# A planner that lays out the opening too, knows the shared port, picks engines, and fills TensorE's gaps with zero products

## The chip, the cores and the metric

The kernel runs on one core of one Trainium2 chip. The metric is the device time of one execution in microseconds (us), the median of several runs. The engines are TensorE (PE, matrix products; PEld is its weight load), VectorE (DVE), ScalarE (ACT), GpSimd (POOL) and SyncE (SP, which here only issues DMAs).

## The reference

An mLSTM layer runs over 4 batches, 8 heads, 768 steps and a head dimension of 40; its output, 3072 rows of 320, goes through a bilinear block of width 1536. All arrays are float32 but the three weight matrices, which come as 8-byte floats.

```
for t in range(S):
    m_new = max(f_gate[t] + m, i_gate[t])
    f_stab = exp(f_gate[t] + m - m_new);  i_stab = exp(i_gate[t] - m_new);  m = m_new
    C = f_stab * C + i_stab * outer(v[t], k[t])
    n = f_stab * n + i_stab * k[t]
    denom = max(abs(n . q[t]), 1)
    y[t] = sigmoid(o_gate[t]) * (C @ q[t]) / denom
x = y as (B*S, H*D)
out = ((x @ w_a) * (x @ w_b)) @ w_out
```

## The kernel before

The recurrence is computed chunkwise: 24 chunks of 128 steps (6 per batch, batches interleaved). For a chunk, `begin_a`/`stage_a` make transposed q and k (tile T), `begin_e`/`stage_e` a matrix of decays (E, tile gbc), `begin_b`/`stage_b` the scores (pS) times E, `begin_i`/`stage_i` the part of the carried state (pI), `begin_c`/`stage_c` the product with v (pV), `stage_u` the state's update (pU from vw), `stage_f` the division and gate (tile osig becomes y) and `stage_d` the transposed result, split in two floats of shorter mantissa (xh, xl). The first six chunks use the `begin_` forms, float32 products; later ones use split bf16.

The bilinear block (`moe_block`) takes the chunks in 9 blocks of 2, 2, 3, 3, 3, 3, 3, 2 and 3 chunks. For each of 12 slices of the width, `up` makes two sums of 8 products (pu, 256 or 384 columns, three PSUM buffers), copies one (g), multiplies it by the other, splits g into gh and gl; `down`, two slices later, adds three products per chunk into pd0, pd1, pd2 (320 columns). The last slice copies pd to o and stores it.

The weights come as 8-byte floats in 32 stages. Each stage is made into two floats in the kernel: `high` and `low` read the raw words (qks and cw), `join` puts them together (DVE), `lead_part` copies the leading part (w), `low_part` subtracts it (DVE). The products of the first block wait for them.

The order of the work is made by a planner, `Plan`. The kernel's code is run against a recorder; each call becomes a `Node` with its engine, an occupancy and a latency from `cost`, and edges from `link`: data, ring buffers of a tile, and, while `plan.pinned` is set, the order as written on each engine. `run` is a list scheduler: per engine the ready node of the best rank goes first; `settle` runs it forward and backward 6 times (TURNS), and `emit` issues every engine's instructions in the best order found. All instructions therefore carry one line number in the profile (L349), and tiles tell them apart. Pinned before were the first loads and the hand-written opening: up to the first two chunks' `stage_d` and the first five weight stages. Behind them, PE, DVE and ACT were free, and every later node came after the last pinned one of its engine.

In `run`, SP's loads share one wire with 8 in flight (LANES). Ten products of zeros (`warm`, in bank pd2) stand at the start to raise TensorE's clock.

Of the kernel before, what the change touches and what calls it, by code (L numbers as in the profile page):

```python
# [22 lines left out]
LANES = 8  # L23

# [75 lines left out]
class Node:  # L100
    __slots__ = (
        "i", "eng", "calls", "occ", "lat", "prev", "next", "table", "acc", "pinned", "at", "done", "xfer",
    )

    def __init__(self, i, eng):
        self.i, self.eng, self.calls, self.prev, self.next = i, eng, [], {}, []
        self.occ = self.lat = self.xfer = 0.0
        self.table, self.acc, self.pinned = None, [], False


class Plan:

    ENGINES = {"tensor": "PE", "vector": "DVE", "scalar": "ACT", "gpsimd": "POOL", "sync": "SP"}
    HOP = 0.07

    def __init__(self, nc):
        self.nc, self.nodes, self.rings, self.pinned = nc, [], {}, True
        for name in self.ENGINES:  # L120
            setattr(self, name, Recorder(self, name))

# [3 lines left out]
    def add(self, engine, op, args, kw):  # L126
        eng = self.ENGINES[engine]
# [12 lines left out]
        if not (  # L140
            eng == "PE" and node is not None and node.eng == "PE" and node.acc[0][0] == okey
            and len(node.calls) < 8 and node.pinned == self.pinned
        ):
            node = Node(len(self.nodes), eng)
            node.pinned = self.pinned
            self.nodes.append(node)
        node.calls.append((engine, op, args, kw))
        node.acc += acc
        self.cost(node, eng, op, out, refs, args, kw)
# [17 lines left out]
    def cost(self, node, eng, op, out, refs, args, kw):  # L167
        cols = int(np.prod(out.shape[1:]))
        size = [x.size if isinstance(x, View) else mybir.dt.size(x.dtype) for x in refs]
        if eng == "PE":  # L170
            if op == "transpose":
                occ = 0.109
            else:
                f32 = [str(x.dtype) if not isinstance(x, View) else x.kind() for x in refs[1:3]]
                if size[1] == 2:
                    occ = cols / 2400 + 0.005 if cols > 64 else 0.026
                elif "float32r" in f32[0]:
                    occ = cols / 2400 + 0.011
                else:
                    occ = 0.108 if refs[1].shape[0] <= 64 else 0.22  # L180
            node.occ += occ
            node.lat = 0.17
        elif eng == "ACT":
# [3 lines left out]
            node.occ = 0.04 + cols * 0.00094 + (0.13 if bias else 0.0)  # L187
            node.occ += 0.05 if "Prelu" in func or "scale" in kw else 0.0
            node.lat = 0.11
        elif eng == "DVE":  # L190
            rate = 960.0
            one = op in ("tensor_copy", "tensor_scalar", "memset") and all(
                not isinstance(x, View) or x.root.ring[0] != "psum" for x in refs
            )
# [4 lines left out]
            node.occ = 0.065 + cols / rate  # L199
            node.lat = 0.085  # L200
        elif eng == "POOL":
            node.occ = 0.1 + cols * (0.0009 if op in ("affine_select", "memset") else 0.002)
            node.lat = 0.1
        elif op == "dma_start_transpose":
            node.occ, node.lat, node.xfer = 1.3, 1.6, 0.0
        else:
            n = int(np.prod(out.shape)) * size[0]
            rows = out.shape[-1] * size[0]
            node.occ, node.lat = 0.47 if rows > 512 else 0.6, 1.7
            node.xfer = n / (340e3 if rows > 512 else 172e3)  # L210

    def link(self):
        last, chain, rings = {}, {}, {}
        for node in self.nodes:
# [22 lines left out]
        for node in self.nodes:  # L237
            if not node.pinned and node.eng in ("PE", "DVE", "ACT"):
                self.edge(chain[node.eng], node, order=True)
# [7 lines left out]
    def edge(self, a, b, order=False):  # L247
        if a is b or (order and a.i in b.prev):
            return
        if a.eng == b.eng and a.eng != "SP":  # L250
            gap = a.occ
            if a.eng in ("DVE", "ACT", "POOL") and not order:
                gap += 0.06
        else:
            gap = a.occ if order else None
        if order and a.eng != b.eng:
            gap = 0.0
        if a.i not in b.prev:
            a.next.append(b)
            b.prev[a.i] = gap  # L260
        elif gap is None or (b.prev[a.i] is not None and gap > b.prev[a.i]):
            b.prev[a.i] = gap

    def run(self, rank, forward=True):
        nodes = self.nodes
        engines = list(dict.fromkeys(self.ENGINES.values()))
        free = dict.fromkeys(engines, 0.7 if forward else 0.0)
        wait = {e: [] for e in engines}
# [4 lines left out]
        table, wire, landed = "E", 0.0, []  # L273
        order = []
        for x in nodes:
            if lack[x.i] == 0:
                heapq.heappush(wait[x.eng], (0.0, rank[x.i], x.i))
        while len(order) < len(nodes):
            best = None
            for e in engines:  # L280
                if ready[e]:
                    t = free[e]
                elif wait[e]:
                    t = max(free[e], wait[e][0][0])
                else:
                    continue
# [3 lines left out]
            while wait[e] and wait[e][0][0] <= t + 1e-9:  # L290
                r, k, i = heapq.heappop(wait[e])
                heapq.heappush(ready[e], (k, i))
            k, i = heapq.heappop(ready[e])
            x = nodes[i]
            if x.table and x.table != table:
                table = x.table
                t += 1.283
            at[i] = t
            free[e] = t + x.occ
            if e == "SP":  # L300
                if forward:
                    if len(landed) >= LANES:
                        t = max(t, landed[-LANES])
                    at[i], free[e] = t, t + x.occ
                    wire = max(wire, t + x.lat) + x.xfer if x.xfer else wire
                    end[i] = wire + 0.35 if x.xfer else t + x.occ + x.lat
                    landed.append(end[i])
                else:
                    free[e] = t + max(x.occ, x.xfer)
                    end[i] = t + x.occ + x.lat + x.xfer  # L310
            else:
                end[i] = t + x.occ + x.lat
            order.append(x)
            for y in x.next if forward else [nodes[j] for j in x.prev]:
                lack[y.i] -= 1
                if lack[y.i] == 0:
                    r = 0.0
                    if forward:
                        for j, gap in y.prev.items():
                            r = max(r, end[j] + self.HOP if gap is None else at[j] + gap)  # L320
                    else:
                        for z in y.next:
                            gap = z.prev[y.i]
                            r = max(r, at[z.i] + z.occ + (y.lat + self.HOP if gap is None else gap - y.occ))
                    heapq.heappush(wait[y.eng], (r, rank[y.i], y.i))
        return order, at, max(end)

    def settle(self):
# [3 lines left out]
        for turn in range(TURNS):  # L332
            order, at, end = self.run(rank)
            if best is None or end < best[1]:
                best = (order, end, at)
            back, late, _ = self.run([-t for t in at], forward=False)
            rank = [-(t + x.occ) for t, x in zip(late, self.nodes)]
# [4 lines left out]
    def emit(self, order):  # L342
# [3 lines left out]
        for node in order:  # L346
            for engine, op, args, kw in node.calls:
                f = getattr(getattr(self.nc, engine), op)
# [7 lines left out]
class Recorder:  # L356

    def __init__(self, plan, name):
        self._plan, self._name = plan, name

    def __getattr__(self, op):
        return lambda *args, **kw: self._plan.add(self._name, op, args, kw)
# [17 lines left out]
def kernel(  # L380
# [395 lines left out]
    def stage_a(n):  # L776
# [10 lines left out]
        for j in range(2):  # L787
            qks = qks2[2 * (n % 2) + j]
            ph, pm, pl = (qks[:, 1, :, at[i][j]:at[i][j] + D] for i in "hml")
            nc.scalar.copy(ph, src[:, j])  # L790
# [3 lines left out]
            (nc.gpsimd if 2 * n + j < 4 else nc.vector).tensor_tensor(r, src[:, j], ph, op=ALU.subtract)  # L794
            nc.vector.tensor_copy(pm, r)
            yield
            (nc.gpsimd if n < 8 else nc.vector).tensor_tensor(pl, r, pm, op=ALU.subtract)
# [21 lines left out]
    def stage_b(n, hf):  # L819
# [14 lines left out]
        nc.scalar.copy(pb[:, 0], E)  # L834
# [115 lines left out]
    def stage_f(n):  # L950
# [15 lines left out]
        (nc.vector if n < NS else nc.gpsimd).tensor_tensor(  # L966
# [4 lines left out]
        (nc.scalar.copy if n < NF32 else nc.vector.tensor_copy)(y[:, DM:], y[:, 2 * P:DM])  # L971
# [5 lines left out]
    def stage_d(n):  # L977
# [15 lines left out]
        nc.scalar.copy(xh[:, :, cols], px)  # L993
# [65 lines left out]
    def moe_block(kb):  # L1059
# [5 lines left out]
        def down(ff):  # L1065
# [13 lines left out]
            if ff == NF - 1:  # L1079
                for t in range(sizes[kb]):  # L1080
# [3 lines left out]
                    nc.scalar.copy(o, pd[t][:, 0:DM])  # L1084
                    nc.sync.dma_start(out[b * S + c * P:b * S + (c + 1) * P, :], o)

        def up(ff):
# [5 lines left out]
            for j in range(2):  # L1093
# [12 lines left out]
                if j == 0:  # L1106
                    g = mpool.tile([P, NTB], F32, tag="acp", name=f"g{kb}_{ff}")[:, 0:NT]
                    (nc.vector.tensor_copy if kb > 0 and ff in [1, 2] else nc.scalar.copy)(g, acc[0])
# [33 lines left out]
    def begin_a(n):  # L1142
# [6 lines left out]
        for j in range(2):  # L1149
# [6 lines left out]
            pool, tag = (ps_at, "pat") if n >= NS or n + j == 0 else (ps_dn, "pd2") if j == 0 else (ps_up, "pu")  # L1156
# [6 lines left out]
            (nc.vector.tensor_copy if j == 1 else nc.scalar.copy)(t, pt)  # L1163
# [99 lines left out]
    plan.pinned = False  # L1263
# [11 lines left out]
    plan.pinned = True  # L1275
# [4 lines left out]
    for _ in range(WARM):  # L1280
        nc.tensor.matmul(warm, idle[:, 0:P], idle, start=True, stop=True)

# [139 lines left out]
```

## Time and profile before

| | |
|---|---|
| median of 3 runs (lowest, highest) | 553.07 us (552.47, 554.78) |
| the profiled execution | 552.61 us, span 550.8 us |
| busy, share of the span | PE 96%, PEld 92%, DVE 74%, ACT 43%, POOL 23% |
| mean granted TensorE clock | 0.966 |
| q, k, v, o_gate loads, 160 KB each | 24 of each |

"Busy" is the share of the span in which an engine had an instruction under way. The clock row of the profile gives the granted clock in tenths of full speed for 40 equal slices of the span, 9 being 90% or more. A name such as pu<-xh,w is output from inputs by the program's tiles.

### The profile page before, as it was taken

The numbers are of one execution on the slowest core, as the hardware profiler recorded it, in microseconds if no ns is written. First come the engines' busy times: TensorE is split into PE (matmuls) and PEld (weight loads), VectorE is DVE, ScalarE is ACT, GpSimd is POOL, SyncE is SP. The second block draws the span as 40 slices with busy tenths as digits, with TensorE's granted clock in tenths as the row PEclk, the third lists the DMA queues.
The fourth block names the chain that finished last, engine by engine and source line by source line (L and its number), as shares of the span: only waits on it lengthen the run. The fifth ranks groups of instructions, "written<-read, shape, count | busy, mean of one in ns | idle before, by whom it ended". The sixth has DMA issues, their size and how long they took to land. (4 is left out here: it accounts for less than half of the span.)

```text
span 550.8 us, 12384 instructions
## 1 busy us (share of the span) xinstructions
PE 529.5 (96%) x4810; PEld 506.3 (92%) x4810; DVE 408.0 (74%) x940; ACT 234.4 (43%) x556; POOL 126.1 (23%) x185
## 2 busy tenths in 40 slices
PE   7787899989999999999999999999999999999997
PEld 5676899989999999999899999999999999999997
DVE  5897875578969985987869985988869856844342
ACT  5689997354523642432623444432432622311111
POOL 2012353453232231242132131232030202000000
PEclk9668799989999999999999999999999999999999
DMA  9999923559767756479745659567635535100001
GB/s 170 304 255 312 163 54 65 150 87 166 149 142 125 159 121 149 96 123 171 134 118 129 100 131 191 91 137 147 120 107 86 115 64 116 38 1 26 1 1 37
DMA packets 198679, 66.77 MB, mean 121 GB/s; under 512 B 184252, under 2 KB 191900, under 8 KB 198620
## 3 DMA queue, kind: packets, MB, share of 16 engines
q1 hardware_dynamic: 198620, 65.98, 58.1%
q8 instruction: 38, 0.62, 0.5%
q14 instruction: 21, 0.17, 0.1%
HBM read 41.11 MB, written 5.97 MB: 85 GB/s over the span
## 5 line engine op out<-in xcount | busy, mean ns | idle before, releaser
L349 PE MATMUL pu<-xh,w 128*128 128x384 f32 (+1 forms) x1080 | 281.5, 328 | 0.6 <-ACT xh L349 0.6
L349 PE MATMUL pu<-xl,w 128*128 128x384 f32 (+1 forms) x648 | 211.9, 329 | 1.0 <-DVE xl L349 1.0
L349 PEld LDWEIGHTS pu<-xh,w 128*128 128x128 f32 x1080 | 195.6, 194 | 1.7 <-ACT xh L349 1.0
L349 PE MATMUL pd<-w,gh 128*128 128x320 f32 x576 | 134.5, 315 | 0.0
L349 PEld LDWEIGHTS pu<-xl,w 128*128 128x128 f32 x648 | 126.0, 194 | 2.1 <-DVE xl L349 1.3
L349 PEld LDWEIGHTS pd<-w,gh 128*128 128x128 f32 x576 | 98.0, 190 | 0.4
L349 DVE TENSOR_TENSOR g<-pu,g 128x384 f32<-128x384 f32 (+1 forms) x108 | 54.7, 507 | 57.9 <-PE pu L349 53.5
L349 PE MATMUL pd<-w,gl 128*128 128x320 f32 x288 | 90.4, 315 | 0.0
L349 ACT COPY g<-pu 128x384 f32<-128x384 f32 (+1 forms) x92 | 40.3, 438 | 96.5 <-PE pu L349 96.3
L349 ACT ACTIVATE gbc<-gbc,gtab 128x128 f32<-128x128 f32 x160 | 54.3, 394 | 20.5 <-POOL gbc L349 20.5
L349 POOL TENSOR_TENSOR vr<-va 128x336 f32<-128x336 f32 x18 | 14.5, 804 | 211.7 <-PE pV L349 211.7
L349 PEld LDWEIGHTS pd<-w,gl 128*128 128x128 f32 x288 | 54.3, 189 | 0.2 <-DVE gl L349 0.2
L349 DVE TENSOR_TENSOR gl<-g,gh 128x384 fp32r<-128x384 f32 (+1 forms) x92 | 51.7, 562 | 1.9
L349 ACT CAST pb<-gbc 128x512 bf16<-128x512 f32 x36 | 22.3, 619 | 45.0 <-DVE gbc L349 44.8
L349 PE MATMUL pV<-va,gbc 128*128 128x42 bf16 (+1 forms) x240 | 36.2, 235 | 1.8 <-ACT T L349 1.8
L349 DVE CAST gh<-g 128x384 fp32r<-128x384 f32 (+1 forms) x96 | 33.9, 353 | 1.7
L349 DVE TENSOR_TENSOR num<-pV,num 128x336 f32<-128x336 f32 x20 | 10.1, 505 | 32.9 <-PE pV L349 32.9
L349 DVE TENSOR_TENSOR gbc<-pS,gbc 128x512 f32<-128x512 f32 x48 | 32.3, 680 | 2.9 <-PE pS L349 2.3
L349 ACT CAST cb<-cst 128x168 bf16<-128x168 f32 x18 | 6.0, 333 | 61.6 <-DVE cst L349 34.2
L349 PE MATMUL pS<-T,T 120*128 120x128 bf16 (+1 forms) x352 | 29.4, 236 | 1.8 <-DVE T L349 1.8
L349 PEld LDWEIGHTS <-T 120*128 120x128 bf16 x576 | 24.7, 97 | 6.4 <-issue 4.1
L349 POOL TENSOR_TENSOR gl<-g,gh 128x256 fp32r<-128x256 f32 x16 | 13.1, 821 | 56.5 <-ACT gh L349 49.7
(102 smaller groups left out, 763.7 us busy)
## 6 DMA issues: line engine op xcount, KB each, us to landing
gbc<-g_dram SPq DMA_DIRECT2D x20, 512.0 KB
qk<-in_q_dram SPq DMA_DIRECT2D x24, 160.0 KB
qk<-in_k_dram SPq DMA_DIRECT2D x24, 160.0 KB
va<-in_v_dram SPq DMA_DIRECT2D x24, 160.0 KB
osig<-in_o_gate_dram SPq DMA_DIRECT2D x24, 160.0 KB
raw<-in_moe_w_out_dram SPq DMA_DIRECT2D x12, 320.0 KB
out_dram<-o SPq DMA_DIRECT2D x24, 160.0 KB
raw<-in_moe_w_a_dram SPq DMA_DIRECT2D x8, 384.0 KB
```

What stands on the lines that cost most here:

```text
L349: f(*[real(x) for x in args], **{k: real(x) for k, x in kw.items()})
```

## The change

The planner is changed, and with it who does some of the operations:

- Nothing is pinned any more: the opening, its loads among it, is ordered by the planner too.
- A node may have several engines (`alts`). `nc.copier` stands for ACT or DVE, `nc.adder` for DVE or POOL; `run` picks one when it schedules the node, and leaves a node for the other engine if that would end it sooner (`better_elsewhere`).
- A DVE instruction marked as using the port (a copy, memset or tensor_scalar outside PSUM, or two inputs, outside PSUM) and a POOL instruction (all but memset) exclude each other in the plan; POOL steps back for a more urgent DVE one (POLITE).
- An engine of AHEAD may leave itself idle for a more urgent node that comes within the ready one's time (SLACK, KEEP).
- PE's cost doubles where the spell of 3.4133 us before had too little PE work; a gap between the first warm product and the first other tile of the bank pd2 is filled with zero products of 256 columns.
- Costs of ACT, POOL, PE and DMA, the hop between engines and the gap between dependent instructions are changed; narrow loads are held to two in flight.
- In `begin_a`, chunk 1's transposed q moves from bank pd2 to the ring pu.

```
+AHEAD = ('DVE', 'ACT', 'PE')
+SLACK = 1.0
+KEEP = 0.2
+POLITE = True
+SPELL = 3.4133
...
-    HOP = 0.07
+    HOP = 0.05
+    DEP = {"DVE": 0.115, "ACT": 0.115, "POOL": 0.11, "PE": 0.0}
...
+        self.copier = Recorder(self, "scalar", "vector")
+        self.adder = Recorder(self, "vector", "gpsimd")
...
-                    occ = cols / 2400 + 0.011
+                    occ = cols / 2400 + 0.0135
...
+            node.use += cols * refs[1].shape[0] * (1 + plain) / 128.0 * out.shape[0] / 128.0
...
+            by[3] = (one or len(refs) > 2) and not any(psum)
...
-            node.occ = 0.1 + cols * (0.0009 if op in ("affine_select", "memset") else 0.002)
+            by[0] = 0.03 + cols * 0.00205
...
-            node.xfer = n / (340e3 if rows > 512 else 172e3)
+            by[2] = n / (305e3 if node.wide else 160e3)
...
-            if node.pinned:
-                if node.eng in chain and node.eng != "POOL":
-                    self.edge(chain[node.eng], node, order=True)
-                chain[node.eng] = node
...
+                if any(q < k - SLACK and r < stop - KEEP and stop - r > r - t for r, q, j in soon):
+                    back.append((k, i))
+                elif len(x.alts) > 1 and better_elsewhere(x, e, t):
+                    back.append((k, i))
...
+            if shared and forward:
+                t = max(t, port[other[e]])
+                port[e] = t + occ - 0.07
+            if e == "PE" and forward:
+                root = x.acc[0][0]
+                if root is self.bank:
+                    filling = True
+                elif root.ring == self.bank.ring:
+                    filling = False
+                z = free[e]
+                while filling:
+                    w = int(z / SPELL)
+                    z += 0.107 if used.get(w - 1, 0.0) >= 0.375 * SPELL * 2400 else 0.214
+                    if z > t:
+                        break
+                    used[w] = used.get(w, 0.0) + 256
+                    order.append(None)
+                w = int(t / SPELL)
+                if used.get(w - 1, 0.0) < 0.375 * SPELL * 2400:
+                    occ = 2 * occ
...
+            if node is None:
+                bank, zero = (real(x) for x in self.filler)
+                self.nc.tensor.matmul(bank, zero[:, 0:128], zero, start=True, stop=True)
+                continue
...
# lead_part, the split of q and k, pb, osig's pad, xh, o, g, gh, T
-            nc.scalar.copy(w[rows, j], W[rows])
+            nc.copier.copy(w[rows, j], W[rows])
...
-            (nc.vector.tensor_copy if kb > 0 else nc.scalar.copy)(gh, g)
+            nc.copier.copy(gh, g)
...
# r and the low part of q and k, osig by den, gl
-            (nc.gpsimd if kb * 12 + ff < 16 else nc.vector).tensor_tensor(
+            nc.adder.tensor_tensor(
...
-            pool, tag = (ps_at, "pat") if n >= NS or n + j == 0 else (ps_dn, "pd2") if j == 0 else (ps_up, "pu")
+            pool, tag = (ps_at, "pat") if n >= NS or n + j == 0 else (ps_up, "pu")
...
+    plan.filler, plan.bank = (warm[:, 0:256], idle[:, 0:256]), warm.root
```

More of the change, by code (lines that the diff above doesn't have):

```diff
@@ L247, in edge, with gap, run @@
     def edge(self, a, b, order=False):
-        if a is b or (order and a.i in b.prev):
-            return
-        if a.eng == b.eng and a.eng != "SP":
[L251 to L264, printed above, removed]
+        if a is not b:
+            if a.i not in b.prev:
+                a.next.append(b)
+                b.prev[a.i] = not order
+            elif not order:
+                b.prev[a.i] = True
+    def gap(self, a, b, data):
+        occ, lat = a.by[a.eng][0:2]
+        if a.eng == b.eng and a.eng != "SP":
+            return occ + (self.DEP[a.eng] if data else 0.0)
+        if data:
+            return occ + lat + self.HOP
+        return occ if a.eng == b.eng else 0.0
+    def run(self, rank, forward=True, fixed=None):
         nodes = self.nodes
-        engines = list(dict.fromkeys(self.ENGINES.values()))
+        engines = list(self.NAMES)
         free = dict.fromkeys(engines, 0.7 if forward else 0.0)
+        if forward:
+            free["ACT"] = 2.1
+        hold = dict.fromkeys(engines, 0.0)
         wait = {e: [] for e in engines}
@@ L272, in run, with put @@
         end = [0.0] * len(nodes)
-        table, wire, landed = "E", 0.0, []
-        order = []
+        done = [False] * len(nodes)
+        when = [None] * len(nodes)
+        turn = dict.fromkeys(engines, 0)
+        table, wire, landed, slim, used = "E", 0.0, [], [], {}
+        port = {"DVE": 0.0, "POOL": 0.0}
+        other = {"DVE": "POOL", "POOL": "DVE"}
+        order, count, filling = [], 0, False
+        def put(x, r):
+            when[x.i] = r
+            if fixed is None:
+                for e in x.alts if forward else (x.eng,):
+                    heapq.heappush(wait[e], (r, rank[x.i], x.i))
@@ new lines, in better_elsewhere @@
+        def better_elsewhere(x, e, t):
+            mine = max(t, port[other[e]] if x.by[e][3] else t) + x.by[e][0]
+            for o in x.alts:
+                if o != e:
+                    b = max(free[o], t) + x.by[o][0]
+                    for k, i in ready[o]:
+                        if k < rank[x.i] and not done[i] and nodes[i].alts[0] == o:
+                            b += nodes[i].by[o][0]
+                    if b < mine:
+                        return True
+            return False
@@ new lines, in choose @@
+        def choose(e, t):
+            back, found = [], None
+            if not forward:
+                return heapq.heappop(ready[e])[1]
+            soon = [(r, k, i) for r, k, i in wait[e] if not done[i] and r < t + 2.0] if e in AHEAD else ()
+            while ready[e] and found is None:
+                k, i = heapq.heappop(ready[e])
+                if done[i]:
+                    continue
+                x = nodes[i]
+                occ = x.by[e][0]
+                stop = t + occ
+                if x.by[e][3]:
+                    stop = max(t, port[other[e]]) + occ
+                if any(q < k - SLACK and r < stop - KEEP and stop - r > r - t for r, q, j in soon):
+                    back.append((k, i))
+                elif len(x.alts) > 1 and better_elsewhere(x, e, t):
+                    back.append((k, i))
+                elif e == "POOL" and x.by[e][3] and any(
+                    q < k - SLACK and not done[j] and nodes[j].by["DVE"][3] for q, j in ready["DVE"]
+                ) and POLITE:
+                    back.append((k, i))
+                else:
+                    found = i
+            for z in back:
+                heapq.heappush(ready[e], z)
+            return found
@@ L275, in run @@
         for x in nodes:
             if lack[x.i] == 0:
-                heapq.heappush(wait[x.eng], (0.0, rank[x.i], x.i))
-        while len(order) < len(nodes):
+                put(x, 0.0)
+        while count < len(nodes):
             best = None
             for e in engines:
[L281 to L284, printed above, removed]
-                else:
-                    continue
+                if fixed is not None:
+                    if turn[e] == len(fixed[e]) or when[fixed[e][turn[e]]] is None:
+                        continue
+                    t = max(free[e], when[fixed[e][turn[e]]])
+                else:
+                    while ready[e] and done[ready[e][0][1]]:
+                        heapq.heappop(ready[e])
+                    while wait[e] and done[wait[e][0][2]]:
+                        heapq.heappop(wait[e])
+                    if ready[e]:
+                        t = max(free[e], hold[e])
+                    elif wait[e]:
+                        t = max(free[e], wait[e][0][0])
+                    else:
+                        continue
@@ L992, in stage_d @@
         cols = slice(t0, t0 + P)
-        nc.scalar.copy(xh[:, :, cols], px)
+        nc.copier.copy(xh[:, :, cols], px)
         yield
```

180 lines of the change are left out of this document (107 added, 73 removed).

## The prediction

> **What bounds the kernel now.** I read the page's first lines, then a table of the span by stage (busy time of each engine, clock granted to TensorE), then the list of what PE waited for.
>
> ```profile
> span 550.8 us, 12384 instructions
> PE 529.5 (96%) x4810; PEld 506.3 (92%) x4810; DVE 408.0 (74%) x940; ACT 234.4 (43%) x556; POOL 126.1 (23%) x185
> PEclk9668799989999999999999999999999999999999
> ...
> 0.00:23.00 23.00, 16.76 (x145) 13.28 (x145) 15.69 (x41) 13.00 (x24) 3.39 (x22) 0.86 1.01 225
> 23.00:45.00 22.00, 18.91 (x126) 17.40 (x127) 18.27 (x34) 16.58 (x38) 2.46 (x5) 0.68 1.03 270
> 45.00:69.00 24.00, 19.19 (x161) 17.19 (x160) 20.12 (x40) 23.15 (x54) 7.54 (x12) 0.79 1.07 229
> 69.00:99.00 30.00, 30.00 (x239) 29.07 (x238) 18.18 (x41) 23.44 (x60) 11.99 (x18) 1.00 0.28 53
> 99.00:152.50 53.50, 50.75 (x495) 48.85 (x494) 42.99 (x105) 23.79 (x67) 21.81 (x28) 0.94 0.77 146
> 152.50:213.40 60.90, 60.90 (x596) 58.31 (x596) 52.17 (x118) 24.84 (x58) 16.91 (x21) 1.00 0.69 137
> 213.40:455.70 242.30, 241.19 (x2275) 231.30 (x2275) 193.24 (x452) 91.83 (x213) 57.01 (x73) 1.00 0.61 121
> ```
>
> A row of the table reads: stretch, its length, then busy microseconds (count) of PE, PEld, DVE, ACT, POOL, then clock, DMA share, GB/s. After 152.5 us PE has no hole worth naming and full clock: the kernel is bound by PE there, and PE's work is fixed by the mathematics. So the end can move only by what PE loses, idle or at half clock, and nearly all of that lies before 152.5 us: idle 23.00 - 16.76 = 6.24, then 3.09, 4.81, 0 and 2.75, together 16.9 us.
>
> The other loss is the clock. The next table is cut where the granted clock changes, each half-clock stretch with the window before it.
>
> ```profile
> 13.09:16.50 3.41, 3.41 (x40) 3.29 (x37) 2.55 (x8) 2.76 (x5) 0.00 (x0) 1.00 1.23 253
> 16.50:30.15 13.65, 9.65 (x45) 8.49 (x45) 11.03 (x24) 8.81 (x22) 0.00 (x0) 0.50 1.04 270
> 30.15:33.57 3.42, 1.87 (x18) 1.27 (x15) 3.26 (x6) 3.41 (x7) 0.00 (x0) 1.00 0.91 217
> 33.57:40.39 6.82, 6.29 (x38) 6.09 (x39) 6.57 (x15) 4.41 (x12) 1.49 (x4) 0.50 1.08 336
> 47.22:50.63 3.41, 0.69 (x4) 0.42 (x4) 2.33 (x6) 3.34 (x7) 0.51 (x1) 1.00 1.05 326
> 50.63:57.46 6.83, 6.54 (x57) 6.15 (x58) 5.91 (x11) 6.81 (x19) 2.71 (x4) 0.50 0.96 220
> 60.88:64.29 3.41, 2.86 (x24) 2.81 (x24) 2.98 (x6) 3.36 (x9) 1.91 (x3) 1.00 1.34 186
> 64.29:67.70 3.41, 3.41 (x28) 3.16 (x28) 3.01 (x9) 3.11 (x9) 1.44 (x2) 0.50 1.11 181
> 115.49:118.90 3.41, 2.12 (x20) 2.03 (x21) 1.93 (x5) 3.01 (x11) 2.14 (x3) 1.00 0.74 142
> 118.90:125.73 6.83, 6.83 (x33) 6.79 (x33) 5.28 (x16) 1.50 (x4) 2.19 (x4) 0.50 1.06 148
> ```
>
> In the five half-clock stretches PE is busy 9.65 + 6.29 + 6.54 + 3.41 + 6.83 = 32.7 us for work that full clock would do in 16.4. The first two, 15.94 us and so 7.97 lost, lie where the new filler products can act; the last three, 16.78 us and 8.39 lost, lie behind it. Idle plus half clock is 16.9 + 16.4 = 33.3 us: that is all there is to win.
>
> ```profile
> PE warm L349 <- DVE idle L349: 3.3, 1, 3.3
> PE pX L349 <- DVE osig L349: 3.1, 3, 2.4
> PE pU L349 <- POOL vw L349: 3.0, 1, 3.0
> PE pI L349 <- DVE gbc L349: 2.3, 1, 2.3
> PE pV L349 <- ACT T L349: 1.8, 1, 1.8
> PE pS L349 <- DVE T L349: 1.8, 1, 1.8
> ```
>
> These are PE's waits (total, times, longest). Each is one attention product of an early chunk standing at the head of PE's queue, while products of the bilinear block are ready behind it. The first, 3.3 us, is the start and stays.
>
> **The change, part by part.**
>
> The filler. Zero products of 256 columns go into the gaps that the plan sees between the first warm-up product and the first tile in bank pd2, which is ptg.
>
> ```profile
> 3.25 3.82 PE L349 MATMUL warm<-idle 128*128 128x512 bf16 x10 [3.25 <-DVE idle L349]
> 22.98 0.58 PE L349 MATMUL pu<-xh,w 128*128 128x256 f32 x1 [0.57 <-ACT xh L349]
> 43.96 0.41 PE L349 MATMUL ptg<-ident,qks 96*128 96x96 f32 x3
> 50.92 1.09 PE L349 MATMUL pU<-vw,qk 128*64 128x42 f32 x16 [3.02 <-POOL vw L349]
> 98.98 0.92 ACT L349 COPY o<-pd 128x320 f32<-128x320 f32 x2 [1.76 <-PE pd L349]
> 498.20 8.32 PE pu L349 x48
> ```
>
> The ten warm-up products are zeros too. The last row, from the chain of waits, is a dense run: 8.32 / 48 = 0.173 us for 384 columns, so some 0.116 for 256 and 0.231 for 512. The warm-up's 3.82 / 10 = 0.38 lies between that and its double: the clock rose while only zeros ran, so zeros count as activity. Up to 45 us PE is busy 16.76 + 18.91 = 35.7 us, at full clock 35.7 - 7.97 = 27.7; of 45 us less the start's 3.25 that leaves 14 us of room, some 120 fillers. Gain: between 0 (the clock stays or PE waits as much longer) and 7.97 us. I take half, 4.0: from 25 to 40 us DVE and ACT are nearly full (3.26 and 3.41 of 3.42 us before 33.57), so half of a faster PE's time turns into waiting for T, g and the weights. Cost: where inputs come sooner than planned, fillers already stand in PE's queue ahead of real work; between 0 and the whole 14 us. I take 1.0, nearest to zero, since the filler stops at the planned start of the next product.
>
> The Trainium skill's page "TensorE: Matmul & The Clock Gate", Part 1, has the array fall to half clock after at least one idle window of about 3.4 us. This trace does not follow it: in the window before 64.29 PE was busy 2.86 of 3.41 us and the clock fell all the same. By that rule no window here would have gone cold, and the sum would lose its 4.0 (rival 5).
>
> The opening laid out. Only the hand order of some first 27 us was pinned (to the last low_part of stage 3); behind it the old plan already chose. New there is that gate work, weight steps, loads (SP's issues too, now ordered by rank) may move past one another. Idle up to 45 us is 6.24 + 3.09 = 9.3, less 3.3 at the start 6.0. Gain from 0 to 6.0, or a loss as large if a load of q, k, v or a gate slips behind weights: SP's queue is served in order and DMA is full there (share 1.01 and 1.03). I take 2.0, the smaller end, because of that DMA share. Moving chunk 1's first transpose from pd2 to the pu ring costs nothing: that ring's earlier tiles are copied out while PE does the products between.
>
> The better due times (dependent waits, hop, port, clock in the plan's PE cost). They act on 45 to 152.5 us: idle 4.81 + 2.75 = 7.56 and half clock 8.39, 15.9 us in three groups, at 50.9 (vw late), 61 to 64 (T late) and 117 (gbc late). Each pays twice, as a wait and as the half-clock stretch behind it. I take half, 8.0: a plan that sees vw or gbc late has dense products to put ahead (PE has no hole from 69 to 99), but the third group hangs on a chain through POOL, ACT and DVE that stays. Ends: 15.9 gained, or 3 lost if one more such wait appears.
>
> The engine choice.
>
> ```profile
> L349 ACT CAST w<-cw 128x384 fp32r<-128x384 f32 x16 | 8.2, 511 | 3.8 <-DVE cw L349 3.8
> L349 DVE CAST gh<-g 128x384 fp32r<-128x384 f32 x72 | 26.0, 361 | 1.4
> L349 DVE TENSOR_TENSOR gl<-g,gh 128x384 fp32r<-128x384 f32 x72 | 42.7, 594 | 1.4
> L349 POOL TENSOR_TENSOR gl<-g,gh 128x256 fp32r<-128x256 f32 x16 | 13.1, 821 | 56.5 <-ACT gh L349 49.7 <-DVE gh L349 4.4 <-DMA g_dram<-qks 2.5
> ```
>
> A copy of a weight from SBUF to SBUF takes 0.51 on ACT and, by the nearest row, 0.36 on DVE; ACT has 23.15 of 24 us in use from 45 to 69, DVE 20.12. Moving 8 of the lead copies there frees ACT 4 us and loads DVE 3. That is how the 8.0 can come about, so it is not counted again. After 152.5 us the choice can win at most 1.1 us (213.4 to 455.7 less 241.19 busy); there gh may go from DVE to ACT (ACT has 150 us free) and gl to POOL, 0.82 for 256 columns and so an estimated 1.23 for 384, instead of 0.59. I take 0, since PE covers it; if the cover goes, it is the rival below.
>
> The sum: -4.0 + 1.0 - 2.0 - 8.0 = -13.0, a span of 537.8. The profiled execution took 552.61 us, 1.8 more than its span, and lies 0.46 under the median of 553.07: so 539.6 for it and 540.0 as a median.
>
> **The rivals.** (1) More: the plan's new model is good, PE wins nearly all of the 33.3 less 3.3 of start and 5 of chains, 25 us: 528 to 533. For it, PE's waits are few and single; against it, ACT's 23.15 of 24 us.
>
> (2) The opening is paced by ACT, DVE and DMA and not by PE: fillers warm a PE that then waits, and 2 us remain, 551. For it the rows of 30.15 to 33.57; against it that from 47.22 to 50.63 PE did 0.69 us of work with weights already converted.
>
> (3) Slower, by the fillers: the plan takes inputs for later than they are, or takes half clock for granted where it is full, and fills the time. All 14 us of fillers stand ahead of ready work, the clock wins 7.97, the layout nothing: 553 + 14 - 8 = 559. It decides from 8 us of fillers that stand before ready work. For it: products run in order, nothing passes a filler. Against: the plan stops each filling at the due time.
>
> (4) Slower, by the port of DVE and POOL in the PE-bound part.
>
> ```profile
> L349 DVE TENSOR_TENSOR r<-qk,qks x36: 472/479/1355, 106.8 to 428.4; 128x320 f32<-128x320 f32 x36
> 109.31 1.10 POOL L349 TENSOR_SCALAR_AFFINE_SELECT gbc<-gbc 128x1024 f32<-128x1024 f32 x1
> 109.40 1.35 DVE L349 TENSOR_TENSOR r<-qk,qks 128x320 f32<-128x320 f32 x1 [0.77 <-POOL cb L349]
> ```
>
> A subtraction that takes 0.48 at the median takes 1.35 when it starts under a POOL instruction: it ends 0.34 after that one. From 213.4 to 455.7 DVE has 242.3 - 193.24 = 49 us free. If 72 gl go to POOL at 1.23 and each holds up one DVE instruction for all of that, DVE loses 89 us and is spared 43: 46 net, just under the 49. With some 36 copies of g, about 0.55 each, moved to DVE as well it is 66, 17 over, and PE waits one for one: 540 + 17 = 557. It decides from 49. For it, DVE is the fullest engine beside PE; against, the new plan prices that port and picks the engine that ends first. The Trainium skill's page "SBUF — State Buffer", Who interferes with whom, calls the port an exclusive lock, where the later one waits in full; the row above agrees.
>
> (5) The clock does not heed the fillers, as it falls only for a whole window without work: then filling short gaps buys no clock, the sum is -9.0 and the time 544. For it nothing but that every stretch here follows a window with some idle time in it; against it the windows before 33.57 and 64.29, with 1.87 and 2.86 of 3.4 us busy. It is the rule of the page named above.
>
> **How the numbers follow.** The forecast 0.51 (533 to 548), rival 5, inside it, 0.04, rival 1 0.13, rival 2 0.13, rival 3 0.11, rival 4 0.08. About 0.5% (550.3 to 555.8) is what a measurement here tells from no change: rival 2 is the same case. Faster 0.68, same 0.13, slower 0.19. The range goes from 529, where most of rival 1 is in, to 556, taking in rival 2 and the near edge of 3 and 4; the rest, about 0.2, is left out.
>
> **What would show it.** Right: the clock is 1.0 from some 7 us to ptg, with a hundred or more zero products; the first product of the bilinear block comes before 22.98; the block's last copies at 98.98 in this trace come some 9 us sooner; PE's waits for vw and gbc are shorter than 3.0 and 2.3; from block 2 on PE is as dense as now. Wrong: PE's waits before 69 us as long as before in sum (rival 2), real products whose inputs were ready long before they ran behind fillers (rival 3), or DVE busy over 95% and PE waiting for gl, xl or g after 152.5 us (rival 4).

## The result and the profile after

| | before | after |
|---|---|---|
| median of 10 runs (lowest, highest) | 555.37 us (552.47, 559.64) | 546.21 us (544.38, 550.68) |
| ratio, 95% interval | | 0.9847 (0.981 to 0.9883) |
| profiled execution | 552.61 us, span 550.8 | 545.67 us, span 543.6 |
| mean granted clock of that execution | 0.966 | 0.994 |

The changed kernel is 1.5% faster, 9.2 us between the medians and 7.2 between the profiled spans (the kernel before had 553.07 us in the three runs shown first, and 555.37 over these ten). The forecast was 540.0 in 529 to 556: right in sign, but the gain is between half and 0.7 of the 13.0 us that stood there. Ratios leave out executions over 1.5% above the fastest of their own kernel, which is one of six in e4, one of twelve in e10 and four of twelve in e8 (with all its runs e8 would be at 1.00).

First the page's lines and the table by stage of the changed kernel, cut as the one of before (stretch, length, busy microseconds and count of PE, PEld, DVE, ACT, POOL, clock, DMA share, GB/s).

```profile
span 543.6 us, 12605 instructions
PE 534.1 (98%) x4919; PEld 508.5 (94%) x4919; DVE 409.1 (75%) x903; ACT 240.2 (44%) x577; POOL 151.4 (28%) x201
PEclk9997999999999999999999999999999999999999
...
0.00:23.00 23.00, 20.45 (x179) 16.91 (x180) 10.80 (x35) 11.60 (x21) 3.41 (x22) 1.00 0.99 216
23.00:45.00 22.00, 21.64 (x199) 19.14 (x198) 21.37 (x46) 18.94 (x45) 0.49 (x3) 1.00 1.03 269
45.00:69.00 24.00, 22.67 (x189) 20.71 (x188) 23.56 (x49) 22.63 (x53) 7.81 (x10) 0.86 0.83 219
69.00:99.00 30.00, 30.00 (x245) 28.61 (x244) 19.33 (x48) 20.68 (x52) 7.53 (x14) 1.00 0.41 81
99.00:152.50 53.50, 52.58 (x560) 50.10 (x560) 45.64 (x107) 26.50 (x74) 24.04 (x29) 1.00 0.64 117
152.50:213.40 60.90, 60.43 (x591) 57.31 (x590) 52.67 (x113) 25.16 (x58) 19.13 (x22) 1.00 0.81 141
213.40:455.70 242.30, 241.71 (x2281) 231.73 (x2282) 193.44 (x418) 96.40 (x233) 84.72 (x98) 1.00 0.64 129
```

PE's idle time up to 152.5 us is 2.55 + 0.36 + 1.33 + 0 + 0.92 = 5.2 us, against 16.9 before. One half-clock stretch is left; the next fence has it with the window before it. PE lost half of 6.71, 3.4 us, against 16.4.

```profile
43.38:46.79 3.41, 2.32 (x22) 1.85 (x21) 3.26 (x8) 3.30 (x9) 0.78 (x1) 1.00 0.84 202
46.79:53.61 6.82, 6.71 (x55) 6.12 (x55) 6.73 (x12) 6.76 (x15) 4.86 (x8) 0.50 0.56 175
```

Idle plus half clock thus fell from 33.3 to 8.6 us, by 24.7, and the span by only 7.2. Of the other 17.5 us some 13.7 are in the zero products; the last 3.8 are not accounted for. The first fence is the table for the tile `warm` (PE alone), the second that tile's own view.

```profile
0.00:45.00 45.00, 17.53 (x119) 1.00 1.01 242
```

```profile
L477 PE MATMUL warm<-idle x109: 272/273/394, 2.5 to 35.5; 128*128 128x256 bf16 x109
```

The warm-up took 3.82 us before; so the 109 fillers fill some 13.7 us. The timeline shows where they stand (start, duration, engine, operation, count of a run of equal ones).

```profile
23.74 0.88 DVE L484 TENSOR_TENSOR osig<-pV,osig 128x320 f32<-128x320 f32 x2
...
21.70 3.12 PE L477 MATMUL warm<-idle 128*128 128x256 bf16 x27
24.65 0.49 PE L484 MATMUL pX<-ident,osig 128*128 128x128 f32 x3
26.15 0.39 PE L484 MATMUL pu<-xh,w 128*128 128x256 f32 x1
...
93.95 0.87 ACT L484 COPY o<-pd 128x320 f32<-128x320 f32 x2 [1.38 <-PE pd L484]
146.41 0.43 ACT L484 COPY o<-pd 128x320 f32<-128x320 f32 x1 [1.45 <-PE pd L484]
540.38 0.43 ACT L484 COPY o<-pd 128x320 f32<-128x320 f32 x1 [0.50 <-PE pd L484]
```

The run of 27 fillers ends as osig lands: DVE's two products with osig end at 24.62, pX starts at 24.65. Here the zeros pass time that PE would have waited (in e1 below, without them, PE waits 2.5 us for osig). The first bilinear product comes at 26.15, 3.2 us later than before. Of the kernel before, block 0's copies stand in the prediction; the same of block 1 and of the last block:

```profile
152.53 0.86 ACT L349 COPY o<-pd 128x320 f32<-128x320 f32 x2 [1.53 <-PE pd L349]
546.66 1.35 ACT L349 COPY o<-pd 128x320 f32<-128x320 f32 x3 [3.98 <-PE pd L349]
```

Block 0's copies start at 93.95 instead of 98.98. Block 1's last one starts at 146.41 instead of 152.53 + 0.43, and the last of all at 540.38 instead of 546.66 + 0.90: 5.0, 6.5 and 7.2 us sooner. Nearly the whole gain is there by block 1.

What PE waits for, in order of total (total, times, longest):

```profile
PE warm L477 <- DVE sides L484: 2.5, 1, 2.5
PE pU L484 <- POOL vw L484: 1.0, 1, 1.0
PE pV L484 <- DVE pb L484: 0.9, 1, 0.9
PE pd L484 <- ACT gh L484: 0.4, 1, 0.4
```

The wait for vw fell from 3.0 to 1.0; those for gbc (2.3) and T (1.8 and 1.8) are gone, and that for osig (3.1) is filled with zeros.

To separate work from being busy, I counted every PE product that is not a zero at the spacing its shape shows in dense full-clock stretches (128x256 0.120 us, 128x384 0.174, 128x320 0.147) and summed by stage:

| us of PE work done in | 0-45 | 45-69 | 69-99 | 99-152.5 |
|---|---|---|---|---|
| before | 25.1 | 11.1 | 29.0 | 45.3 |
| after | 24.4 | 16.6 | 27.8 | 48.7 |
| e1, zeros left out | 23.2 | 15.1 | 27.8 | 46.2 |
| e2, before with fillers | 25.1 | 10.2 | 26.6 | 45.4 |
| e4, old engines | 23.1 | 16.2 | 29.2 | 47.9 |
| e5, no port in the plan | 24.5 | 9.7 | 27.9 | 48.8 |
| e12, longer fillers | 22.7 | 13.2 | 29.4 | 47.5 |
| e13, 12 turns | 23.8 | 14.9 | 27.4 | 45.2 |

The opening did 0.7 less, the next 24 us 5.5 more, then -1.2 and +3.4: together 7.0 of the span's 7.2. So the gain shows behind the opening. Each row is of one execution.

### The profile page after: what moved, and what is told of

The parts are those of the page before. It is cut to its first block, busy times and chain, and to the rows that moved or that the text cites. A ratio compares the mean times of both kernels' runs of the same rounds, so it can differ in the third digit from the quotient of the medians.

```text
span 543.6 us, 12605 instructions
## 1 busy us (share of the span) xinstructions
PE 534.1 (98%) x4919; PEld 508.5 (94%) x4919; DVE 409.1 (75%) x903; ACT 240.2 (44%) x577; POOL 151.4 (28%) x201
## 4 chain that ended last, share of the span: by engine, by line
PE 74%; DVE 12%; SPq 5%; DMA 4%; ACT 2%; issue 2%; DVEq 0%; ACTq 0%
PE pu L484 42%; PE pd L484 19%; SPq L484 5%; PE pV L484 5%; PE pS L484 4%; DVE qks L484 3%; DMA qk<-in_q_dram 2%; DVE gbc L484 2%; PE pI L484 2%; DVE w L484 2%; PE pU L484 2%; DVE pb L484 1%; PE pX L484 1%; DMA raw<-in_moe_w_a_dram 1%; DMA gbc<-g_dram 1%
## 5 line engine op out<-in xcount | busy, mean ns | idle before, releaser
L484 PE MATMUL pu<-xh,w 128*128 128x384 f32 (+1 forms) x1080 | 276.0, 323 | 0.2 <-DVE w L484 0.2
L484 PE MATMUL pu<-xl,w 128*128 128x384 f32 (+1 forms) x648 | 208.5, 324 | 0.0
L484 PEld LDWEIGHTS pu<-xh,w 128*128 128x128 f32 x1080 | 190.5, 189 | 1.4 <-DVE w L484 0.5
L484 PEld LDWEIGHTS pu<-xl,w 128*128 128x128 f32 x648 | 122.7, 189 | 0.9 <-DVE xl L484 0.2
L484 ACT COPY g<-pu 128x384 f32<-128x384 f32 (+1 forms) x98 | 43.6, 445 | 119.3 <-PE pu L484 118.0
L484 ACT CAST gh<-g 128x384 fp32r<-128x384 f32 (+1 forms) x51 | 23.5, 462 | 47.6 <-DVE g L484 47.4
L484 POOL TENSOR_TENSOR gl<-g,gh 128x256 fp32r<-128x256 f32 (+1 forms) x22 | 22.0, 1001 | 50.3 <-ACT gh L484 34.0
L484 DVE TENSOR_TENSOR gbc<-gbc,pb 128x512 f32<-128x512 f32 x36 | 31.8, 884 | 0.2 <-ACT pb L484 0.2
L484 DVE TENSOR_TENSOR pb<-gbc 128x512 bf16<-128x512 f32 x36 | 30.6, 849 | 0.3
L484 PEld LDWEIGHTS <-T 120*128 120x128 bf16 x576 | 24.7, 97 | 6.4 <-issue 4.1
L484 DVE COPY qks<-qks 128x640 bf16<-128x640 bf16 (+1 forms) x72 | 26.9, 382 | 0.0
```

The costliest lines, as they stand in the source:

```text
L484: f(*[real(x) for x in args], **{k: real(x) for k, x in kw.items()})
```

## The experiments

Theory A: the gain is the order behind 45 us that the planner's new model finds. Rivals: F, the zero products (clock); O, the free opening; E, the engine choice. The ratio of each run is to the kernel before, which ran beside it.

### Each part undone: fillers, opening, engines

**e1_no_filler_issued**: the plan and the order of every engine are those of the changed kernel; the zeros are planned, but not issued.

```
             if node is None:
-                bank, zero = (real(x) for x in self.filler)
-                self.nc.tensor.matmul(bank, zero[:, 0:128], zero, start=True, stop=True)
                 continue
```

> The changed kernel with the same planned order, but its 109 zero products are left out. Theory A (up to 45 us the loads, DVE and ACT pace the work, the fillers only occupy time in which PE would wait, and the whole gain comes from the order after 45 us): half clock returns between 15 and 45 us, the first block's last copies stay within 1.5 us of 93.95, ratio to the kernel before 0.983 to 0.990. Rival B (the full clock from the fillers carries the gain): block 0 ends 4 to 8 us later, ratio 0.993 to 1.000.

**e3_pinned**: the opening is held in the hand-written order again, with its old engines.

```
+            if node.pinned:
+                if node.eng in chain and node.eng != "POOL":
+                    self.edge(chain[node.eng], node, order=True)
+                chain[node.eng] = node
...
+        if self.pinned:
+            alts = alts[:1]
```

> The changed kernel with the opening pinned again as written by hand, on its old engines (first loads, first two chunks, first five weight stages); all else as changed, fillers too. Theory A: the free layout of the opening is worth nothing or a little less than nothing, as the first bilinear product came 3.2 us later with it: first pu near 23 us, ratio 0.980 to 0.988. Rival C (the free opening carries part of the gain): ratio 0.989 to 0.996.

**e4_fixed_engines**: each copy and subtraction goes to the engine it had before; all else as changed.

```
-            nc.copier.copy(w[rows, j], W[rows])
+            nc.scalar.copy(w[rows, j], W[rows])
...
-            nc.copier.copy(gh, g)
+            (nc.vector.tensor_copy if kb > 0 else nc.scalar.copy)(gh, g)
```

> The changed kernel with every copy and subtraction on the engine it had before; all else as changed. Theory A: what counts is when the planner thinks an input is ready, not the engine: ratio 0.982 to 0.990. Rival D (the engine choice frees ACT between 45 and 90 us and carries the gain): ratio 0.992 to 1.000, PE's waits for vw or T back at 2 to 3 us.

| | ratio (95%) | median | profiled span, clock |
|---|---|---|---|
| after | 0.9847 (0.981 to 0.9883) | 546.21 | 543.6, 0.994 |
| e1 | 0.9875 (0.9826 to 0.9923) | 549.53 | 548.0, 0.975 |
| e3 | 0.9872 (0.9826 to 0.9918) | 548.58 | 546.7, 0.991 |
| e4 | 0.9818 (0.9775 to 0.986) | 546.22 | 544.2, 0.994 |

All three keep most of the gain, so none of fillers, free opening and engine choice carries it alone. A share of it is not excluded: taking both intervals together, what is lost without the part can be up to 0.9% for the fillers, 0.8% for the opening and 0.3% for the engines. e1 shows what the zeros do. Its clock row and the start of its block 0's copies:

```profile
PEclk9688899988999999999999999999999999999999
...
96.62 0.87 ACT L482 COPY o<-pd 128x320 f32<-128x320 f32 x2 [1.39 <-PE pd L482]
```

Without them the opening runs at half clock from 17.6 to 31.2 us; with them the clock is full until 46.79. Zero products do hold the clock. Without them block 0's copies come 2.7 us later than in the changed kernel, but still 2.4 before the old kernel's; that is more than the 1.5 us of Theory A and less than the 4 to 8 of rival B. Over the whole run the difference is 0.28% of the time, 1.5 us, by the ratios, and 4.4 us between the two profiled spans. By work done the same order has 23.2 us at 45 us without the zeros and 24.4 with them, and 112.3 and 117.5 at 152.5: the zeros do bring some work forward.

e3 missed its forecast of a first bilinear product near 23 us: it came at 27.01. Its second osig was complete with its padding at 23.94, and the product that reads it started at 25.95, behind a run of 26 zeros. So e3 tests the hand order together with zeros that stand ahead of ready work, and says little of the free opening by itself.

### One part alone: fillers, and the new costs, in the old kernel

**e2_before_filler**: the old planner and order, with zeros in the gaps that it planned up to ptg (and chunk 1's transpose moved to the ring pu, so that bank pd2 is free).

```
+            if e == "PE" and forward:
+                root = x.acc[0][0]
+                if root is self.bank:
+                    filling = True
+                elif root.ring == self.bank.ring:
+                    filling = False
+                z = free[e] + 0.107
+                while filling and z <= t:
+                    order.append(None)
+                    z += 0.107
```

> The kernel before, its own order, with zero products of 256 columns issued in the gaps of its plan from the first warm product to ptg (120 of them; one transpose of chunk 1 moves from pd2 to pu as in the change). Theory A: the clock is full up to 44 us, the first block's last copies within 2 us of 98.98, ratio 0.996 to 1.003. Rival B: 4 to 8 us gained, ratio 0.985 to 0.993.

Measured 1.0018 (0.9985 to 1.0052), span 554.2: nothing. The table by stage, PE's waits and the start of block 0's copies:

```profile
0.00:23.00 23.00, 19.75 (x190) 16.58 (x191) 13.23 (x37) 11.62 (x21) 3.37 (x22) 1.00 0.98 237
23.00:45.00 22.00, 21.21 (x202) 19.30 (x200) 20.48 (x38) 17.32 (x41) 3.00 (x5) 1.00 1.01 258
45.00:69.00 24.00, 18.55 (x152) 16.51 (x152) 20.30 (x40) 23.51 (x57) 7.47 (x12) 0.76 1.05 234
```

```profile
PE pU L365 <- POOL vw L365: 3.0, 1, 3.0
PE pI L365 <- DVE gbc L365: 2.3, 1, 2.3
```

```profile
102.38 0.92 ACT L365 COPY o<-pd 128x320 f32<-128x320 f32 x2 [1.77 <-PE pd L365]
```

The clock is 1.0 for the whole opening, where it was 0.86 and 0.68, and PE does the same 25.1 us of work there as before. Its waits for vw and gbc are as long as they were, and block 0 ends 3.4 us later. The faster PE gained nothing, but not because its inputs come when they did before: the zeros stand ahead of real products. The chunks' first transposes (pT), in the old kernel and in e2, and what DVE then waits for:

```profile
6.91 1.04 PE L349 MATMUL pT<-ident,qk 128*128 128x128 f32 x8
```

```profile
7.58 1.58 PE L361 MATMUL warm<-idle 128*128 128x256 bf16 x13
9.00 0.60 PE L365 MATMUL pT<-ident,qk 128*128 128x128 f32 x4
10.51 0.69 DVE L365 COPY T<-pT 128x512 f32<-128x512 f32 x1 [3.75 <-PE pT L365]
```

They start 2.1 us later, and the first bilinear product comes at 25.96 instead of 22.98. By 45 us the full clock has won back what the zeros cost. So e2 shows that these zeros are worth nothing in the old order; it does not show that a full clock is.

**e7_before_new_costs** and **e7b_before_pe_costs**: the old planner with the new costs (all of them, or PE's alone), and no other part of the change.

```
-    HOP = 0.07
+    HOP = 0.05
...
-                    occ = cols / 2400 + 0.011
+                    occ = cols / 2400 + 0.0135
```

> The kernel before (hand opening, fixed engines, no fillers, no port, no half clock in the plan) with all the new costs of PE, ACT, POOL, DMA, hop and dependent gap. Theory A1 (the costs alone carry the gain): ratio 0.983 to 0.991, PE's waits for vw, T and gbc under 1.5 us each. Rival F (the scheduler's new rules carry it: looking ahead, choosing, the half clock in the plan): ratio 0.995 to 1.003.

> The kernel before with only PE's costs new: float32 attention products at 0.108 and 0.052 us where the old plan had 0.22 for most, and 2.5 ns more for a bilinear product. Theory A2 (the old plan held the early chunks' float32 products, which the trace shows at 0.11 us, for twice as long, and so asked for attention inputs too late): ratio as the one with all new costs, within 0.4%. Rival G (the costs of loads, ACT, POOL and the hop matter as much): ratio at least 0.5% above that one.

Measured 1.0012 (0.9985 to 1.0039) and 0.9999 (0.9969 to 1.0029): nothing, so Theories A1 and A2, by which the costs alone carry the gain, fell. PE's waits in e7 moved to other tiles without shrinking:

```profile
PE pE L362 <- ACT gbc L362: 2.6, 1, 2.6
PE pI L362 <- DVE gbc L362: 2.1, 1, 2.1
PE pV L362 <- ACT T L362: 2.0, 1, 2.0
```

### What the plan must know: port and clock

**e5_no_port**: the port of DVE and POOL is taken out of the plan; engines stay free. **e10_fixed_noport** is the same with the old engines.

```
-            if shared and forward:
+            if shared and forward and False:
...
-POLITE = True
+POLITE = False
```

> The changed kernel whose planner no longer knows that DVE and POOL exclude each other at their port. Theory A (the gain is in the order between 45 and 152 us, set by the plan's costs): ratio 0.981 to 0.990. Rival E (port knowledge carries it): ratio 0.992 to 1.000, more DVE instructions stretched to twice their time and PE waits of 1 us and more behind them.

> The changed kernel with every operation on its old engine and with a planner that does not know the port of DVE and POOL. Theory J (the port matters because the planner may send work to POOL; with the old engines it loads POOL little): ratio 0.980 to 0.990, as with fixed engines and the port known. Rival K (the port matters for the order whatever the engines): ratio 1.000 or more.

| ratio (95%) | port in the plan | port not in the plan |
|---|---|---|
| engines chosen by the plan | 0.9847 (0.981 to 0.9883) | 1.0278 (1.0235 to 1.032) |
| engines as before | 0.9818 (0.9775 to 0.986) | 0.9984 (0.9946 to 1.0022) |

e5 fell outside what Theory A (0.981 to 0.990) and rival E (0.992 to 1.000) had forecast, and e10 outside Theory J. With a free choice of engines the port decides 4.3% of the time; with the old engines 1.7%. The span of e5 is 568.3 us, 24.7 above that of the changed kernel. By the work done 6.6 of it are lost up to 152.5 us (110.9 against 117.5), net all of that from 45 to 69; the other 18 lie in the PE-bound part. Its table by stage and its waits:

```profile
152.50:213.40 60.90, 57.01 (x533) 54.08 (x532) 50.33 (x102) 22.56 (x54) 28.47 (x32) 0.97 0.76 131
213.40:455.70 242.30, 235.34 (x2182) 222.45 (x2181) 194.68 (x419) 88.53 (x217) 91.88 (x106) 0.99 0.65 127
```

```profile
PE pd L482 <- DVE gh L482: 4.6, 3, 2.1
PE pS L482 <- DMA T<-qks: 2.7, 3, 1.6
```

From 213.4 to 455.7 us PE does 2182 products where the changed kernel does 2281 in the same time. DVE is not full, 194.68 of 242.3 us; single instructions are late, as PE's waits for gh tell, though the waits listed make up only part of the 18. One copy in the groups of e5 and of the changed kernel (count | busy, mean ns | idle before):

```profile
L482 DVE COPY qks<-qks 128x640 bf16<-128x640 bf16 x36 | 18.4, 520 | 0.0
```

```profile
L484 DVE COPY qks<-qks 128x640 bf16<-128x640 bf16 x36 | 15.3, 428 | 0.0
```

**e8_plan_full_clock** and **e11_fixed_full_clock** (old engines): the plan takes PE's clock for full everywhere; the zeros are laid at the full-clock pace.

```
                 if used.get(w - 1, 0.0) < 0.375 * SPELL * 2400:
-                    occ = 2 * occ
+                    pass
```

> The changed kernel whose planner takes full clock for granted (no doubled PE cost, fillers counted at 0.107). Theory A: the clock's place in the plan is worth little: ratio 0.981 to 0.990. Rival H (seeing the half clock is what keeps the order good from 45 to 152 us): two or more half-clock stretches back in that part and a ratio of 0.991 to 1.000.

> The changed kernel with every operation on its old engine and a planner that takes full clock for granted; port known. Theory L (the half clock in the plan, worth 1.1% with free engines, is what the gain with fixed engines rests on too): ratio 0.990 to 1.000. Rival M (look-ahead, port and costs together carry it): ratio 0.980 to 0.987.

Measured 0.9956 (0.9914 to 0.9998), 1.1% behind the changed kernel, and 0.9993 (0.9954 to 1.0032), 1.75% behind e4. In its trace e8 has two half-clock stretches behind 45 us, 13.7 us in all, where the changed kernel has one of 6.8, as rival H had said.

**e13_turns12**, the control: the planner unchanged, but settled over 12 turns instead of 6, which gives another order.

```
-TURNS = 6
+TURNS = 12
```

> A control: the changed kernel with 12 turns of the planner in place of 6, which gives another order of about the same planned end. It shows how much one plan differs from another of the same planner. Theory A: within 0.5% of the changed kernel, ratio 0.980 to 0.990. Rival N (the gain is the luck of one order): ratio outside 0.978 to 0.993.

Measured 0.9936 (0.9901 to 0.9971), 0.9% behind the changed kernel, though nothing that the planner knows was touched. That is outside Theory A's 0.980 to 0.990 and, by a hair, outside the 0.993 from which rival N (the luck of one order) was to hold. By work done this order gains 2.1 us from 45 to 152.5 us over the kernel before, where the changed kernel gains 7.7; the half clock is back from 120.4 to 127.2 us. So a good part of the gain hangs on which order the planner ends in. A step of about 1% between two plans (e8) is no evidence on a single part, and those of 1.7% (e10, e11) are thin evidence. Only e5's 4.3% is far outside.

All plans together say more than any one step. The five that know port and clock (the changed kernel, e3, e4, e12 below, e13) lie at 0.982 to 0.994, all five intervals below 1; the four that lack one of them (e5, e8, e10, e11) at 0.996 to 1.028. The two groups do not overlap, though e8 and e13 lie within each other's intervals.

### A longer clock: is full clock worth time by itself?

**e12_fixed_long_filler**: e4 with ptg, pdec and the early pU moved from bank pd2 to the ring pat, so that the zeros may reach on to block 2, from a tile of their own.

```
-            pt = ps_dn.tile([P, 512], F32, tag="pd2", name="ptg")
+            pt = ps_at.tile([P, 512], F32, tag="pat", name="ptg")
...
-    idle = apool.tile([P, H * DV], F32, tag="vr", name="idle").bitcast(BF16)[:, 0:512]
+    idle = wpool.tile([P, 256], BF16, name="idle")
```

> A try at a better version: old engines, port and half clock in the plan, and ptg, pdec and the early pU moved from bank pd2 to the attention's ring, so that the bank stays with the fillers to block 2 and they reach over the half-clock stretch near 47 to 54 us (190 of them; the zeros lie in a tile of their own, the warm-up is 20 products of 256 columns). If that stretch costs its 3.4 us: ratio 0.974 to 0.980. If fillers only occupy waiting time, as Theory A says: 0.980 to 0.988.

Measured 0.9847 (0.9804 to 0.989), median 547.71, in the range of Theory A. Its table by stage, and the same stage for the tile `warm` alone:

```profile
45.00:69.00 24.00, 24.00 (x229) 20.86 (x229) 18.57 (x36) 22.54 (x52) 8.48 (x11) 1.00 0.93 220
```

```profile
45.00:69.00 24.00, 8.71 (x68) 1.00 0.93 220
```

The clock is 1.0 in all of its runs and PE never idles in this stage, and there is no gain: 8.71 of the 24 us are zeros, and the work done is 13.2 us, less than the 16.2 of e4 and the 16.6 of the changed kernel, both at clock 0.86. DVE is busy for 18.57 us there, 21.70 in e4, so the zeros, or the tiles moved to another ring, may have held real products back as in e2; that was not told apart. It only scatters less: 546.73 to 548.40 over 6 runs, against 544.38 to 550.68 over 10.

## Why the prediction was right in sign and too large in size

The sum had four terms; the runs size them so.

- **Filler, -4.0 for the clock and +1.0 for its cost.** The mechanism was right: the clock is 1.0 from 5.8 to 46.8 us with 109 zeros, ptg starting at 42.2. The size stays open: leaving the zeros out (e1) costs 1.5 us by the ratios and 4.4 between the two profiled executions, and the intervals take in both nothing and the 3.0 net that stood. In the stage where the clock was to pay, little arrived: by 45 us the same order has done 24.4 us of work with zeros and 23.2 without, 1.2 us for the 4.0. "I take half" was too much there, since PE waits for osig, T and the weights; the prediction's own row from 30.15 to 33.57, DVE 3.26 and ACT 3.41 of 3.42, spoke for less. The cost was not always small either: in the old order (e2) the zeros cost as much as the clock won.
- **Free opening, -2.0.** By 45 us the work done is 0.7 less than before, and 1.9 less without the zeros (e1); the first bilinear product comes at 26.15, not before 22.98. So the opening itself lost where it was to win. Whether its order pays later is open: the ratio with the opening pinned (e3) is 0.25% worse, inside the interval. For the opening this is rival 2; its total was wrong, because the rest was won later.
- **Better due times, -8.0.** By work done the stages from 45 to 152.5 us give 5.5 - 1.2 + 3.4 = 7.7 us, and the waits for vw, gbc and T shrank as forecast. That the size fits is in part luck: the same planner in another order (e13) gives 2.1 there, with old engines (e4) 7.9. What was not foreseen: of the three half-clock stretches behind 45 us only two went, and a stretch from 46.8 to 53.6 stayed, behind a window where PE had 2.32 of 3.41 us. Which part of the planner brings this term is less clear than the term: the new costs alone bring nothing, and port and clock in the plan are shown as a group only.
- **Engine choice, 0; after 152.5 us, 0.** Both right: e4 equals the changed kernel, and PE has 241.71 us from 213.4 to 455.7, 241.19 before. But with free engines the zero holds only with the port in the plan, as e5 shows.

By work done, +0.7 up to 45 us, where the sum had -5.0, and -7.7 behind make -7.0, which is what the span shows (7.2). So the step that failed is the gain in the opening, and the time came inside the range because the term behind it held in this order. Block 0 was to end some 9 us sooner; it ended 5.0 sooner, as part of the gain (3.4) lies behind 99 us.

The other rivals. (1) did not come: its 25 us were all idle and half clock turned into work, and of the 24.7 us that did go, 13.7 went into zeros. The prediction's "all there is to win" counted time in which PE could work, not time for which it had inputs. (3) came in e2 and in e3, where zeros stand ahead of ready products: in e2 the clock was won and given back, block 0 later by 3.4 us; no more than that. (4) came in e5, by another route than worked out. It was to decide once DVE loses its 49 free us; DVE kept 242.3 - 194.68 = 48 us free and 4.3% was lost all the same. PE's waits for gh suggest why: a late instruction holds PE up whether or not the engine is full on average. (5) fell: with the zeros the clock stays up, without them (e1) it falls. What the prediction had for it was misread, too: not every half-clock stretch follows a window with idle time, as in its own first row, 13.09 to 16.50, PE is busy for all 3.41 us and the clock falls. Busy time alone does not tell here when it will.

On that last point the Trainium skill's page "TensorE: Matmul & The Clock Gate", Part 1, asks for an idle window before the half clock. The fall at 46.79 us follows a window that was 68% busy (2.32 of 3.41), so the trace does not agree here either.

What stays open: how much of the 1.5% is the planner's knowledge and how much the luck of one order (0.9%, e13), and, with the old engines, how the 1.7% of the port (e10) and the 1.75% of the clock in the plan (e11) share the gain; they do not add up, since there each one taken out costs nearly all of it. Only one other order of the very same planner was run. Splitting the copies of T between ACT and DVE again under the free plan was not tried.

## What to carry to other kernels

Idle or half-clock time of the bounding engine is a gain only as far as its inputs are ready: before pricing a filler or a clock, look at what its feeders (here DVE and ACT) have left in that very stretch, and take little where that is little. Zeros also cost, wherever they stand ahead of products whose inputs came sooner than planned; to size them, leave them out of an unchanged order (e1), as adding them to another one (e2) shows both effects at once. A planner that may choose engines must know what the engines share; without the port its freedom cost 4.3%, and an engine that is 80% busy on average can still be the one that is late. Before crediting a part of a scheduler with 1%, run the same scheduler with an arbitrary change of its order: here that alone moved the time by 0.9%.

## What the runs showed of the hardware

The time at half clock differs from one execution of the same program to the next: the changed kernel's runs have mean clocks of 0.984 to 0.994 and spans of 548.5 to 542.3 us to match, while e12, at 1.0 in every run, spans 544.9 to 546.6. A full clock went with a steadier time here, not with a shorter one. Zero products of 256 columns hold the clock up: with 109 of them it is 1.0 from 5.8 to 46.8 us, without them half from 17.6 to 31.2. The port stretches DVE's copy of 128x640 in the changed kernel too: 26 of its 36 copies run with no POOL instruction beside them and take 0.31 us, the other ten 0.72 on average; without the port in the plan it is 14 of 36, at 0.84.
